# New order, engine and buffer tables for a hand-scheduled attention and SoLU kernel

## The chip, the cores and the metric

The kernel runs on one core of one Trainium2 chip. The metric is the time of one execution on the device in microseconds (us); the median of several runs counts. The engines are TensorE (PE, matmul; PEld is its weight load), VectorE (DVE), ScalarE (ACT), GpSimd (POOL) and SyncE (SP, which issues most of the transfers).

## What is computed

Attention with batch 4, 8 heads, 768 positions and head size 64, in which each position sees its last 96 positions and the first 8 ones, with a bias by distance and head; and then on its 3072 rows of 512 a feed-forward layer of width 1024 with a SoLU and a normalization. Cut to what matters:

```python
scores = q @ k.T / sqrt(64) - slope[head] * distance      # per batch and head
scores = where(local or first 8, scores, -1e9)
x = softmax(scores) @ v                                   # -> [3072, 512], all heads side by side
h = x @ w_in                                              # [3072, 1024]
solu = h * softmax(h)
ln = (solu - mean(solu)) / sqrt(var(solu) + 1e-6) * g_ln
out = ln @ w_out                                          # [3072, 512], float32
```

## The kernel before

The program is cut into 714 steps. Python code creates them with their dependencies (`Plan.step`), each with the engine or the engines that may do it. Four tables near the top of the file then decide: `ORDER` is the order in which all steps are written out, so each engine gets its own steps in that order and works through them in order; `SLOTS` gives each step the buffers that it takes; `ENGS` picks the engine of a step that has a choice; and `WARM` puts matmuls on constant data (L1292, tile busy) in front of some PE steps, where `20:2:13` means thirteen ahead of entry 20 of the order, into bank 2. `Plan.order` applies the tables. Waits follow from the dependencies and from who has the buffer.

For each of the 4 batches:

- q and k of a head pair are loaded (L523, tile x), cast to float16 (tile x again; L275 on ACT, L277 on DVE, L279 on POOL), transposed on PE (L785) and copied to kT and qT. For the last batch a transposing transfer does this (L530).
- A *scores* step makes the products of one head pair and half of the positions (L941), with the bias added by a matmul for batch 0 (L927). ACT takes the exponential (L949, tile eb). For batches 1 to 3 the bias is a factor instead, multiplied in by DVE or POOL (L959). The factor (tile fb) is made once by eight exponentials (L322) from distances and slopes (sf, L317).
- gscores and gexp do the first 8 positions (L998, L1013). *sums* adds up the weights (L1027), ACT takes the logarithm (L1044), DVE splits it (L1051), *spread* spreads it over the partitions (L1073), and ACT takes the reciprocal by an exponential (L1085, tile rr). av1 and av2 multiply by v (L1121), with a small copy (tick, L1129) between them, and DVE multiplies by rr to give xT (L1141).

For each of the 24 tiles of 128 rows: the first product gemm1 (L1174, 16 matmuls with their loads), the exponential ef (L1180, ACT), uu = ef * h (L1183, DVE), its squares (sq; L1190 on ACT or L1194 on DVE), a transpose of uu (L1209 on PE with a copy to tile late, or a transposing transfer, L1199), the second product gemm2 (L1266), the scaled output osb (L1276 on ACT, L1279 on DVE) and its store (L1283).

The weights: w_in is loaded in four pieces (L658, tile late) and cast in eight (w_in_sb). w_out is loaded in four pieces (L668), each of its eight blocks is scaled by g (gw; L681 on ACT, L683 on POOL, L687 on DVE), a product with a constant gives the mean over the rows (L694), and DVE subtracts it (L698, "centred"). The first gemm2 needs all eight centred blocks.

PE's results lie in eight banks of one tile, acc. A step takes one bank ("one") or a pair of banks ("big"), and gives it back when another engine has read it: a scores step's pair after ACT's exponential, a gemm1's pair only after ACT's exponential and DVE's uu, a gemm2's bank after the scaled output. In the code, for gemm1:

```python
g1 = step("PE", 1728, tt, xt_st[t] + w_in_st, None, take=("big", "ef"), mode="f", ...)
u = step("DVE", 1140, tt + 3000, [ex], None, take="uu", free=[g1], lat=113, name="u")
```

Of the kernel before, what the change touches and what calls it, by code (L numbers as in the profile page):

```python
# [30 lines left out]
FACT = {1, 2, 3}  # L31
SPLIT = False
ORDER = """
# [29 lines left out]
"""  # L63
SLOTS = """
# [10 lines left out]
"""  # L75
ENGS = """
# [5 lines left out]
"""  # L82
WARM = """
20:2:13 32:2:5 45:2:2 54:2:1 82:0:3 100:0:1 110:6:1 139:5:1 171:4:2
"""


# [1243 lines left out]
```

## Time and profile before

| what | before |
|---|---|
| median of 3 runs | 159.84 us (159.53 to 160.11) |
| the profiled execution's own time | 158.12 us |
| its span | 156.5 us, 4929 instructions |
| busy: PE, DVE, ACT, POOL | 144.1, 119.9, 123.8, 51.9 us |
| transfers | 35.83 MB, mean 229 GB/s |
| granted clock of TensorE | 1.00 over the span |

The profile is of one execution; its span leaves out what lies around the program. A busy time of PE includes the modelled ends of matmuls that overlap. "Idle before" names what ended the wait.

### The profile page before, as it was taken

To read this page: it belongs to the slowest core of one execution; us is meant where nothing else is said; L and a number is where in the kernel's file an instruction comes from. 1 tells how busy PE (TensorE), PEld (TensorE's weight loads), DVE (VectorE), ACT (ScalarE), POOL (GpSimd) and SP (SyncE) were. 2 spreads that over 40 slices of the span, in tenths; PEclk is the share of its full clock that TensorE was granted. 3 is DMA by queue.
4 is the path that set the end of the run, shared out by engine and by line. 5 is a ranking of instruction groups with operands and counts; after the bars stand their busy time and mean duration, and the time that the engine had idled before them with its cause. 6 is when DMAs were issued, how large, how long until landed. Compare 5 with 4: busy or idle time off the path is not lost.

```text
span 156.5 us, 4929 instructions
## 1 busy us (share of the span) xinstructions
PE 144.1 (92%) x1974; PEld 76.3 (49%) x1974; DVE 119.9 (77%) x249; ACT 123.8 (79%) x214; POOL 51.9 (33%) x120
## 2 busy tenths in 40 slices
PE   6998986997898999999998999999989799999991
PEld 2455553456454546556544456454444454445460
DVE  6966553799879998889999997499777462788840
ACT  3389986999996999758996998989999546589712
POOL 7705714189438521734960000448301000000000
PEclk9999999999999999999999999999999999999999
DMA  4997899999969999999999899999999983054684
GB/s 157 335 351 178 288 311 397 366 272 329 266 161 264 213 202 294 204 275 201 219 239 176 182 237 216 164 263 135 215 225 290 211 316 133 4 113 89 188 315 168
DMA packets 74317, 35.83 MB, mean 229 GB/s; under 512 B 63344, under 2 KB 69816, under 8 KB 74296
## 3 DMA queue, kind: packets, MB, share of 16 engines
q1 hardware_dynamic: 73576, 34.36, 92.8%
q10 hardware_dynamic: 720, 1.18, 2.0%
q8 instruction: 15, 0.25, 0.6%
q14 instruction: 6, 0.05, 0.1%
HBM read 23.15 MB, written 6.29 MB: 188 GB/s over the span
## 4 chain that ended last, share of the span: by engine, by line
PE 34%; DMA 21%; DVE 16%; SPq 13%; ACT 7%; issue 4%; POOL 3%; DVEq 0%; ACTq 0%; POOLq 0%
PE acc L1266 11%; PE acc L1174 10%; SPq L537 5%; DVE uu L1183 5%; DMA x<-in_k_dram 4%; DVE eb L959 4%; DMA x<-in_q_dram 4%; DMA kT<-x 4%; DMA vgn<-vgn 4%; PE acc L1121 4%; DMA out_dram<-w_out 3%; DVE sqv L1194 3%; SPq L523 3%; SPq L1199 3%; PE acc L785 2%
## 5 line engine op out<-in xcount | busy, mean ns | idle before, releaser
L1174 PE MATMUL acc<-w_in_sb,xT 128*128 128x512 f16 x192 | 44.0, 380 | 1.3 <-POOL w_in_sb L279 1.3
L1266 PE MATMUL acc<-gw_out_sb,late 128*128 128x512 f16 (+1 forms) x200 | 44.7, 371 | 0.0
L1183 DVE SCALAR_TENSOR_TENSOR uu<-ef,acc 128x1024 f16<-128x1024 f16 x24 | 29.1, 1216 | 6.3 <-ACT ef L1180 4.5
L949 ACT ACTIVATE eb<-acc 128x960 f16<-128x960 f32 (+1 forms) x32 | 29.3, 944 | 1.3 <-PE acc L941 1.1
L1180 ACT ACTIVATE ef<-acc 128x1024 f16<-128x1024 f32 x24 | 24.6, 1025 | 6.9 <-PE acc L1174 6.1
L1174 PEld LDWEIGHTS <-xT 128*128 128x128 f16 x192 | 17.8, 98 | 21.5 <-DVE g L625 1.2
L1266 PEld LDWEIGHTS <-late 128*128 128x128 f16 x200 | 18.4, 98 | 20.1 <-issue 0.6
L279 POOL CAST x<-x 128x768 f16<-128x768 f32 x19 | 17.0, 898 | 30.0 <-DMA qT<-x 17.0
L1141 DVE TENSOR_TENSOR xT<-acc,rr 128x768 f16<-128x768 f32 x16 | 15.1, 954 | 5.9 <-ACT rr L1085 4.5
L1276 ACT ACTIVATE w_out<-acc,rstd 128x512 f32<-128x512 f32 (+1 forms) x19 | 12.7, 678 | 7.5 <-PE acc L1266 4.3
L1190 ACT ACTIVATE sqa<-uu 128x1024 f16<-128x1024 f16 x14 | 14.8, 1058 | 1.8 <-DVE uu L1183 1.7
L959 DVE TENSOR_TENSOR eb<-eb,fb 128x960 f16<-128x960 f16 (+1 forms) x21 | 14.8, 735 | 0.0
L1085 ACT ACTIVATE rr<-acc 128x768 f32<-128x768 f32 x16 | 12.2, 805 | 2.9 <-PE acc L1073 2.8
L785 PE MATMUL acc<-ident,x 128*128 128x128 f16 x144 | 11.3, 220 | 2.1 <-POOL x L279 1.1
L1194 DVE SCALAR_TENSOR_TENSOR sqv<-uu 128x1024 f16<-128x1024 f16 x10 | 12.6, 1265 | 0.1
L1121 PE MATMUL acc<-eb,v 64*64 64x160 f16 (+2 forms) x448 | 12.5, 217 | 0.0
L1292 PE MATMUL acc<-busy 128*128 128x512 f16 x29 | 10.3, 485 | 1.5 <-DVE busy L598 1.5
L785 PEld LDWEIGHTS <-x 128*128 128x128 f16 x144 | 8.6, 98 | 5.6 <-POOL x L279 1.5
L1121 PEld LDWEIGHTS <-v 64*64 64x64 f16 x448 | 10.2, 107 | 2.2 <-issue 1.7
L941 PE MATMUL acc<-qT,kT 64*64 64x160 f16 (+2 forms) x384 | 10.8, 227 | 0.3 <-ACT qT L275 0.3
L279 POOL CAST v<-v 128x704 f16<-128x704 f32 (+3 forms) x13 | 6.9, 555 | 11.9 <-DMA v<-in_v_dram 11.9
L1121 PE MATMUL acc<-eg,vgz 64*64 64x192 f16 x128 | 9.2, 257 | 0.0
(113 smaller groups left out, 189.1 us busy)
## 6 DMA issues: line engine op xcount, KB each, us to landing
x<-in_k_dram SPq DMA_DIRECT2D x16, 384.0 KB, 5.8
x<-in_q_dram SPq DMA_DIRECT2D x16, 384.0 KB, 4.8
out_dram<-w_out SPq DMA_DIRECT2D x19, 256.0 KB, 2.9
v<-in_v_dram SPq DMA_DIRECT2D x12, 192.0 KB, 5.3
late<-in_moe_w_in_dram SPq DMA_DIRECT2D x4, 512.0 KB, 4.5
w_out<-in_moe_w_out_dram SPq DMA_DIRECT2D x4, 512.0 KB
v<-in_v_dram SPq DMA_DIRECT2D x12, 160.0 KB, 3.4
v<-in_v_dram SPq DMA_DIRECT2D x12, 96.0 KB, 6.9
```

What stands on the lines that cost most here:

```text
L279: nc.gpsimd.tensor_copy(out=out, in_=in_)
L785: nc.tensor.transpose(out=pt[:, ts(j, P)], in_=a[:, j], identity=ident)
L949: ex["fn"] = (lambda ex=ex, qk=qk, gw=gw: nc.scalar.activation(out=eb[at(qk, "eb")][:, :, 0:gw], in_=big(qk)[:, :, 0:gw], func=AF.Exp, sca ...
L959: eng.tensor_tensor(out=e, in0=e, in1=fb[:, p, :, 0:gw], op=ALU.mult)
L1121: nc.tensor.matmul(out=o_[:, gl : gl + m], lhsT=lhsT, rhs=rhs, start=(ph == 0 and (d, h) not in done), stop=(ph == 1 and last[d, h] == n), ...
L1141: nc.vector.tensor_tensor(out=xT[at(xt_own[b], "xT")][:, p : p + 2, q0:q1], in0=big(av)[:, :, 0:w], in1=rr[at(re, "rr")][:, :, 0:w], op=AL ...
L1174: nc.tensor.matmul(out=ph()[:, ts(fh, 512)], lhsT=xT[at(xt_own[b], "xT")][:, j, ts(t % NA, P)], rhs=w_in_sb[:, j, ts(fh, 512)], start=(j = ...
L1180: ex["fn"] = lambda g1=g1, t=t, ph=ph: nc.scalar.activation(out=ef[at(g1, "ef")], in_=ph(), func=AF.Exp, accum_out=s0[:, t : t + 1])
L1183: u["fn"] = lambda u=u, g1=g1, t=t, ph=ph: nc.vector.scalar_tensor_tensor(out=uu[at(u, "uu")], in0=ef[at(g1, "ef")], scalar=USC, in1=ph(), ...
L1190: nc.scalar.activation(out=sqs_["ACT"], in_=uu[at(u, "uu")], func=AF.Square, accum_out=s2[:, t : t + 1])
L1194: nc.vector.scalar_tensor_tensor(out=sqs_["DVE"], in0=uu[at(u, "uu")], scalar=1.0, in1=uu[at(u, "uu")], op0=ALU.mult, op1=ALU.mult, accum_ ...
L1266: nc.tensor.matmul(out=one(g2)[:, 0:wd], lhsT=uT[at(el_o, "uT")][:, c, :], rhs=gw_out_sb[:, c, sl_], start=(c == 0), stop=(c == NFC - 1))
```

## The change

In a few words: all orders, engines and buffers searched anew with a model in which TensorE's instruction fetches queue behind transfers. In the file only the four tables differ; the steps, their dependencies, the number of buffers, and what is computed stay as they are. The tables' rows tell a reader little; one or two lines of each:

```diff
 ORDER = """
-12 3 14 4 79 0 81 8 86 11 126 13 5 24 66 1 73 53 110 7 82 20 88 18 15 60 16 112 36 92 17 83 89 68 90
...
+3 14 13 4 15 12 60 2 0 53 99 92 86 17 62 115 66 16 18 1 24 23 101 63 8 102 19 110 126 73 55 5 94 56
...
 SLOTS = """
-0 0 0 2 3 2 4 0 1 5 1 3 4 0 0 2 2 5 0 0 0 1 2 1 2 0 1 2 5 0 6 0 2 2 7 2 10 0 0 1 4 6 0 3 3 0 1 1 1 1
...
+0 1 2 3 4 0 0 0 5 1 1 2 3 1 0 2 5 1 3 4 0 3 0 2 1 0 1 3 2 1 2 3 0 7 0 0 3 3 1 1 1 2 2 6 2 2 1 0 1 3
...
 ENGS = """
-0 0 0 1 0 2 1 2 1 1 0 2 1 1 1 1 0 1 0 0 1 0 1 1 2 1 0 2 2 2 1 1 2 2 0 0 1 1 0 1 0 2 0 0 0 1 0 1 0 1
...
+0 0 0 0 1 2 1 0 0 0 0 0 1 1 0 0 0 1 0 1 0 2 1 0 0 0 1 2 2 2 2 2 1 1 1 1 1 1 1 0 0 2 0 0 2 1 0 1 0 1
...
 WARM = """
-20:2:13 32:2:5 45:2:2 54:2:1 82:0:3 100:0:1 110:6:1 139:5:1 171:4:2
+23:6:13 25:6:6 34:6:2 46:7:4 47:0:1 57:7:1 66:7:2 73:4:1 110:6:4 116:4:2
 """
```

What the engine table does, by kind of step (ACT / DVE / POOL):

| step | before | change |
|---|---|---|
| cast of k and q (x) | 5 / 8 / 19 | 5 / 4 / 23 |
| copy to kT and qT | 15 / 9 / - | 11 / 13 / - |
| cast of v | 2 / 10 / 12 | 3 / 10 / 11 |
| cast of w_in | 3 / 1 / 4 | 1 / 2 / 5 |
| scaling of w_out (gw) | 3 / 3 / 2 | 1 / 7 / 0 |
| factor (L959) | - / 21 / 3 | - / 18 / 6 |
| squares | 14 / 10 / - | 17 / 7 / - |
| copy of a turned uu | 1 / 6 / - | 2 / 5 / - |
| scaled output | 19 / 6 / - | 15 / 10 / - |

Of POOL's factors one was in batch 1 and two in batch 3; now three are in batch 1, one in batch 2 and two in batch 3. WARM holds 29 matmuls before, two of them behind the first gemm1, and 36 now, all ahead of it.

What the order and buffer tables do to some PE steps of batches 1 to 3 (by step number; "held by" is who had the banks last, and what frees them; the count is of PE steps from the holder to the step):

| PE step | before: held by, freed by | change: held by, freed by |
|---|---|---|
| scores 357 | gemm1 774, uu (6) | scores 345, exponential (4) |
| scores 513 | gemm1 857, uu (3) | scores 501, exponential (3) |
| scores 672 | gemm1 954, uu (6) | scores 666, exponential (4) |
| sums 697 | gemm2 922, output on ACT (4) | gemm2 922, output on DVE (8) |
| scores 348 | scores 357, exponential (3) | gemm1 774, uu (5) |
| scores 498 | gemm1 823, uu (11) | gemm1 830, uu (6) |
| scores 510 | two turned q, copies (4) | gemm1 857, uu (7) |

Three places in the order, as the built programs have it.

SP, the first loads. Before, from the seventh x load to the last w_out load (x are pieces of q and k, v and vt of v, vgn the first 8 rows, late w_in):

```order
L523 DMA x_0_101<-in_k_dram 128x2x384
L523 DMA x_2_103<-in_q_dram 128x2x384
L537 DMA v_1_112<-in_v_dram 128x3x64
L545 DMA vt_89<-in_v_dram 64x4x64 x2
L537 DMA v_2_113<-in_v_dram 128x3x64
L537 DMA v_0_111<-in_v_dram 128x3x64
L537 DMA v_1_112<-in_v_dram 128x3x64
L537 DMA v_0_111<-in_v_dram 128x3x64
L537 DMA v_2_113<-in_v_dram 128x3x64
L552 DMA vgn<-in_v_dram 64x1x64
L658 DMA late<-in_moe_w_in_dram 128x1024 x4
L668 DMA w_out_71<-in_moe_w_out_dram 128x2x512 x4
```

In the change, from the first w_in load on (the eighth x load stands four rows ahead of this piece):

```order
L658 DMA late<-in_moe_w_in_dram 128x1024 x2
L545 DMA vt_89<-in_v_dram 64x4x64
L552 DMA vgn<-in_v_dram 64x1x64
L537 DMA v_2_113<-in_v_dram 128x3x64
L552 DMA vgn<-in_v_dram 64x1x64
L658 DMA late<-in_moe_w_in_dram 128x1024
L537 DMA v_0_111<-in_v_dram 128x3x64
L537 DMA v_2_113<-in_v_dram 128x3x64
L537 DMA v_0_111<-in_v_dram 128x3x64
L658 DMA late<-in_moe_w_in_dram 128x1024
L537 DMA v_1_112<-in_v_dram 128x3x64
L668 DMA w_out_71<-in_moe_w_out_dram 128x2x512
```

Three of the four w_in loads moved ahead of v pieces. Behind this piece a v piece, a w_out load, a k load of the next batch and the last two w_out loads follow; before, no other load stood between the last w_in and the last w_out.

ACT, its first rows. Before:

```order
L596 ACT_TABLE_LOAD
L275 CAST x_0_107<-x_0_101 128x768
L275 COPY kT_116<-acc 128x768
L275 CAST x_0_107<-x_1_102 128x768
L275 COPY qT_123<-acc 128x768
L275 COPY kT_117<-acc 128x768
L949 ACTIVATE eb_132<-acc 128x960
```

In the change:

```order
L596 ACT_TABLE_LOAD
L275 CAST x_0_107<-x_0_101 128x768
L322 ACTIVATE fb<-dm,sf 128x160 x8
L275 COPY kT_116<-acc 128x768
L275 COPY qT_121<-acc 128x768
L949 ACTIVATE eb_130<-acc 128x2x448
```

The factor's eight exponentials (L322), which stood behind the first three ef of batch 0, are now the second work of ACT.

DVE, from the second xT of batch 0 to the last centred block. Before:

```order
L1141 TENSOR_TENSOR xT_99<-acc,rr_147 128x2x384
L625 COPY g_73<-acc 128x8
L687 TENSOR_SCALAR gw_out_sb<-w_out_71,g_73 128x512 x3
L1183 SCALAR_TENSOR_TENSOR uu_151,s_93<-ef_148,acc 128x1024
L1183 SCALAR_TENSOR_TENSOR uu_152,s_93<-ef_149,acc 128x1024
L277 COPY late<-acc 128x1024 x2
L1183 SCALAR_TENSOR_TENSOR uu_153,s_93<-ef_150,acc 128x1024
L698 SCALAR_TENSOR_TENSOR gw_out_sb<-w_out_71,g_73,acc 128x512 x6
```

In the change:

```order
L1141 TENSOR_TENSOR xT_99<-acc,rr_147 128x2x384
L277 COPY fb<-fb 128x8x320
L687 TENSOR_SCALAR gw_out_sb<-w_out_71,g_73 128x512 x4
L1183 SCALAR_TENSOR_TENSOR uu_152,s_93<-ef_150,acc 128x1024
L687 TENSOR_SCALAR gw_out_sb<-w_out_71,g_73 128x512 x3
L1183 SCALAR_TENSOR_TENSOR uu_151,s_93<-ef_149,acc 128x1024
L1183 SCALAR_TENSOR_TENSOR uu_154,s_93<-ef_148,acc 128x1024
L698 SCALAR_TENSOR_TENSOR gw_out_sb<-w_out_71,g_73,acc 128x512 x2
L277 COPY late<-acc 128x1024
L698 SCALAR_TENSOR_TENSOR gw_out_sb<-w_out_71,g_73,acc 128x512 x3
```

Seven scalings of w_out stand on DVE where three stood, two uu now stand behind the last of them, and one copy of a turned uu instead of two stands among the centred blocks.

## Rows read from the trace of the kernel before

**Rows 1.** The page's first part: busy time, share of the span, instructions.
```profile
PE 144.1 (92%) x1974; PEld 76.3 (49%) x1974; DVE 119.9 (77%) x249; ACT 123.8 (79%) x214; POOL 51.9 (33%) x120
```

**Rows 2.** Table by stage: length; busy PE, PEld, DVE, ACT, POOL; clock; DMA share; GB/s.
```profile
0.00:25.40 25.40, 21.09 (x351) 11.60 (x352) 17.08 (x55) 18.08 (x25) 13.04 (x68) 1.00 0.87 279
25.40:40.40 15.00, 13.85 (x195) 8.21 (x195) 11.89 (x22) 14.40 (x29) 7.64 (x13) 1.00 1.05 336
40.40:60.00 19.60, 18.14 (x219) 9.12 (x216) 18.14 (x29) 17.69 (x31) 10.10 (x13) 1.00 1.03 221
60.00:80.00 20.00, 20.00 (x338) 11.80 (x335) 17.97 (x33) 16.39 (x27) 11.68 (x16) 1.00 1.15 236
80.00:130.80 50.80, 48.64 (x745) 24.29 (x742) 39.80 (x82) 42.35 (x76) 9.48 (x11) 1.00 1.11 221
```

**Rows 3.** Timeline of PE: start, length, instruction, count, idle before and what ended it.
```profile
25.36 5.34 PE L1174 MATMUL acc<-w_in_sb,xT 128*128 128x512 f16 x24 [1.26 <-POOL w_in_sb L279]
...
32.66 1.89 PE L694 MATMUL acc<-gw_out_sb,onesm 128*128 128x512 f16 x8
...
40.37 1.89 PE L1266 MATMUL acc<-gw_out_sb,late 128*128 128x512 f16 x8
...
43.16 0.84 PE L785 MATMUL acc<-ident,x 128*128 128x128 f16 x12 [0.57 <-POOL x L279]
...
50.66 0.22 PE L927 MATMUL acc<-bw,identb 64*64 64x64 f16 x2 [0.50 <-DVE uu L1183]
...
56.19 0.62 PE L1209 MATMUL acc<-ident,uu 128*128 128x128 f16 x8 [0.39 <-DVE uu L1183]
...
83.00 0.22 PE L927 MATMUL acc<-bw,identb 64*64 64x64 f16 x2 [0.59 <-DVE uu L1183]
...
115.56 0.22 PE L927 MATMUL acc<-bw,identb 64*64 64x64 f16 x2 [0.71 <-DVE uu L1183]
...
123.90 0.63 PE L1027 MATMUL acc<-eb,onesd 128*32 128x384 f16 x24 [0.86 <-ACT w_out L1276]
...
144.31 8.82 PE L1266 MATMUL acc<-gw_out_sb,late 128*128 128x512 f16 x48
```

**Rows 4.** The page's third part: the queue of PE's instructions; packets, MB, share.
```profile
q8 instruction: 15, 0.25, 0.6%
```

**Rows 5.** Timelines of POOL and ACT, where they wait for the weights' loads.
```profile
22.87 2.44 POOL L279 CAST w_in_sb<-late 128x512 f16<-128x512 f32 x4 [3.66 <-DMA late<-in_moe_w_in_dram]
30.57 2.04 POOL L683 TENSOR_TENSOR gw_out_sb<-w_out,g 128x512 f16<-128x512 f32 x2 [5.26 <-DMA w_out<-in_moe_w_out_dram]
...
24.67 0.62 ACT L275 CAST w_in_sb<-late 128x512 f16<-128x512 f32 x1 [0.73 <-DMA late<-in_moe_w_in_dram]
```

**Rows 6.** Timeline of ACT: its first copy, two scalings of w_out, the factor.
```profile
7.37 0.80 ACT L275 COPY kT<-acc 128x768 f16<-128x768 f16 x1 [2.55 <-PE acc L785]
...
25.97 1.33 ACT L681 ACTIVATE gw_out_sb<-w_out,g 128x512 f16<-128x512 f32 x2 [0.69 <-DMA w_out<-in_moe_w_out_dram]
...
32.64 2.66 ACT L322 ACTIVATE fb<-dm,sf 128x160 f16<-128x160 f32 x8
```

**Rows 7.** Timeline of DVE, 27 to 40 us.
```profile
27.22 0.49 DVE L687 TENSOR_SCALAR gw_out_sb<-w_out,g 128x512 f16<-128x512 f32 x1 [2.24 <-DMA w_out<-in_moe_w_out_dram]
...
29.62 1.22 DVE L1183 SCALAR_TENSOR_TENSOR uu<-ef,acc 128x1024 f16<-128x1024 f16 x1
...
31.90 1.49 DVE L277 COPY late<-acc 128x1024 f16<-128x1024 f16 x2
...
34.59 4.04 DVE L698 SCALAR_TENSOR_TENSOR gw_out_sb<-w_out,g,acc 128x512 f16<-128x512 f32 x6
...
39.34 0.74 DVE L698 SCALAR_TENSOR_TENSOR gw_out_sb<-w_out,g,acc 128x512 f16<-128x512 f32 x1
```

**Rows 8.** Line L959 (the factor): duration ns min/median/max, first and last start.
```profile
L959 DVE TENSOR_TENSOR eb<-eb,fb x21: 612/650/1987, 47.5 to 121.7; 128x960 f16<-128x960 f16 x11, 128x896 f16<-128x896 f16 x10
L959 POOL TENSOR_TENSOR eb<-eb,fb x3: 1875/2002/2273, 47.0 to 108.9; 128x896 f16<-128x896 f16 x2, 128x960 f16<-128x960 f16 x1
```

82 rows, old and new, of tables (ENGS, ORDER, SLOTS) are left out of this document.

## Prediction

> **What bounds the kernel now.** I read the totals first, then the table by stage, then TensorE's own rows with what ended each of its idle times, and last the rows of the engines that those waits name.
>
> TensorE (PE) is busy for 144.1 us of the span of 156.5 [rows 1]. By stage it is the bound in the middle: 20.00 of 20.00 us from 60 to 80 us, 48.64 of 50.80 from 80 to 130.8 [rows 2]. The end cannot move by itself: the last group of products starts at 144.31 us and runs through without a wait [rows 3], and the tail of the change holds the same products and transposes. So the kernel gains what PE no longer waits, and loses what it waits anew. Ahead of 25.4 us PE's 21.09 busy us [rows 2] hold the warm-up products, so its share says little there; the first product on the tokens starts at 25.36 us, after a wait of 1.26 us for the last cast piece of the first weight [rows 3]. From 25.4 to 40.4 ScalarE (ACT) has 14.40 of 15.00 us busy and VectorE (DVE) 11.89; from 40.4 to 60 DVE has 18.14 of 19.60 [rows 2].
>
> Behind the start-up, PE has five waits [rows 3]: 0.50, 0.59 and 0.71 us before a scores step (L927) for a uu of DVE, 0.39 us before a transpose (L1209) for its own uu, and 0.86 us before sums (L1027) for a scaled output of ACT. They add up to 3.05 us.
>
> **Part 1: the fetches.** The words of the change speak of PE's instruction fetches. The trace shows 15 packets of them, 0.25 MB [rows 4], and each idle row of PE that I found ends with a semaphore of ACT, DVE or POOL (GpSimd) [rows 3]. No idle time is left for a fetch to have caused, so both bounds of this term are 0. The Trainium skill, page "Runtime: NRT & Kernel Launch", section "Instruction fetch mechanics", says that an engine's sequencer fetches the next 16 KiB block over a queue of its own while the current one runs, so that the fetch is mostly hidden. By that rule the term is 0 as well, against the ground that the change gives for itself; how long a fetch stood in its queue no row shows.
>
> **Part 2: up to the first product (25.36 us).** SP issues the loads in another order, but ahead of the last w_in load stand the same pieces: eight x loads, eight v pieces, two vt, two vgn, three w_in. So it has the same bytes before it and lands at about 24.6 us again, where ACT's last cast had waited 0.73 us for it [rows 5]. It can land earlier: from 0 to 25.4 us the transfers ran at 279 GB/s, from 25.4 to 40.4 at 336 [rows 2], and three of the four w_in loads are now queued earlier, so the queue runs dry less. Half of that difference over the 15 us from 10 to 25 is (336 - 279) / 279 / 2 x 15 = 1.5 us, which I take as the most. Behind the landing POOL now casts three halves in a row (2.44/4 = 0.61 us each [rows 5], 1.8 us), where two engines shared them. The first product then starts between 24.6 + 1.8 = 26.4 and 24.9 us; I take 25.8, later by 0.4.
>
> The eight exponentials that build the factor (L322, 2.66 us) move from 32.64 us, in ACT's fullest stretch, to the second place on ACT, where it had been idle for 2.55 us ahead of 7.37 [rows 6]. Their input sf moves up on POOL with them. That idle time is the cover; without it ACT's first copy of kT, and all behind it, comes up to 2.66 us later, which would also show at the first product.
>
> **Part 3: from there to 44 us.** The mean of the second weight (L694) started at 32.66 us [rows 3]. It waited for POOL, which scaled two pieces in 2.04 us from 30.57 on, when their load had landed [rows 5]. Now DVE scales seven of the eight pieces, ACT one and POOL none; of the last load one is DVE's (0.49 us [rows 7]) and one ACT's (1.33/2 = 0.7 us [rows 6]), side by side. In the queue a k load of 384 KB and two v pieces (160 KB) now come ahead of the last w_out load: 0.54 MB, 1.6 us at 336 GB/s, against the up to 1.5 us of part 2. I take the same 30.57. The mean then starts at 30.6 + 0.7 + 0.2 = 31.5 us, 1.2 earlier. The three products ahead of it take 5.3 us [rows 3], from 25.8 to 31.1, and do not hold it.
>
> DVE is next: the first second product (L1266, 40.37 us [rows 3]) needs all eight centred pieces (L698). After its last scaled piece, at 31.1 us, DVE has two uu (1.2 each), eight centred pieces (4.04/6 = 0.67 each) and one copy of a turned tile (1.49/2 = 0.7) [rows 7]: 2.4 + 5.4 + 0.7 = 8.5, so 39.6 us, where the last centred piece ended at 39.34 + 0.74 = 40.1 [rows 7]. That is 0.5. Six instead of five transposed x tiles now stand ahead of that product, so the wait of 0.57 us for POOL at 43.16 us [rows 3] loses its place. Together 1.1 to 1.2 us; I take 1.2. ACT does not bound this stretch any more: it loses the 2.66 us and two scalings (1.4), and takes over one tile copy and two x casts. If the w_out load lands 1.6 us later, DVE ends at 41.2 and the part costs 0.5 us; if it lands 1.5 us earlier, the part gains 2.2.
>
> **Part 4: the rest.** The table of banks in the section on the change shows what four of the five later waits hung on. Three scores steps took banks that a first product had held, so they stood behind ACT's exponential and DVE's uu; now each takes banks that only the exponential of an earlier scores step frees. The sums step took the bank of a second product four PE steps before; now it is eight. So 0.50 + 0.59 + 0.71 + 0.86 = 2.66 us [rows 3] lose their cause. What is late next: other steps now stand behind a uu, as the same table shows for scores steps 348, 498 and 510; 348 most, with the least PE work between. I put three new waits at the mean of the five, 3.05/5 = 0.61: 1.8 us. Net -0.8; the bounds are -2.7 (no new wait) and +2.0 (the slower rival).
>
> The seven more warm-up products (36 for 29) stand ahead of the first product, where PE waits for others, and cost 0; if that cover were gone, each is a product of 512 columns, 5.34/24 = 0.22 us [rows 3], 1.6 us in all. The squares, outputs and casts that change engines count where an engine bounds; PE bounds after 60 us, so I cost them at 0 there. If ACT or DVE fell behind, they would show as new waits, which part 4 holds.
>
> **Sum.** -1.2 (part 3, which swallows the +0.4 of part 2) and -0.8 (part 4): -2.0 on a span of 156.5, so 154.5 us, and 156.1 for the profiled execution, whose own time is 158.12. The median of the three runs is 159.84, 1.72 above it; there the forecast is **157.8 us**. About 0.3% (0.5 us) is what a measurement can tell from no change.
>
> **Rivals.**
> - *More is gained.* No new wait takes the place of the four (-2.7) and the w_out load lands early (-1.8): -4.5, 155.3 us. For it speaks that the four waits have lost their cause; against it, that three steps now stand behind a uu. Chance 0.18.
> - *Nothing is gained.* The w_out load lands 1.6 us later (+0.5) and new waits leave -0.5 of part 4: 159.8 us. This is also the case in which the change does only what its words say, where the trace shows nothing to gain. Chance 0.14.
> - *Slower: POOL's factors.* POOL multiplies six score tiles by the factor instead of three. One takes POOL 1.88 to 2.27 us; DVE's take 0.65 as a median and 1.99 at the longest [rows 8], so the two engines stretch each other. It decides from 40.4 to 60 us, where DVE is nearly full [rows 2] and POOL has three factors for one. If two of DVE's multiplies there are stretched by 1.99 - 0.65 = 1.34 us, 2.7 us of DVE come late, each uu behind them holds its banks longer, and PE has five more waits of 0.6 us (2.9) on top of the three: part 4 is -2.7 + 1.8 + 2.9 = +2.0. Part 3 keeps half, -0.6: +1.4, 161.2 us. Two stretched multiplies are the point; with one the forecast holds. Chance 0.22. The Trainium skill, page "SBUF — State Buffer", section "Who interferes with whom", says that a DVE instruction with two SBUF inputs contends with a GpSimd instruction that reads SBUF, and that one of the two is blocked in full. The 1.99 us agrees with that; by this rule each pair that meets is such a case.
>
> **How the numbers follow.** The forecast (156.8 to 159.3) has the remaining 0.46. Faster by over 0.3% is 0.46 + 0.18 = 0.64, within 0.3% 0.14, slower 0.22. The range goes from 155.8, half way into the larger gain, to 160.9, most of the way into the slower case.
>
> **What would show it.** Right: L694 starts near 31.5 us and the first L1266 near 39.8; the three scores waits for uu and that of L1027 are gone from their steps; the last group of products starts near 142.3. Part 3 is wrong if the scaling on DVE shows a longer wait for w_out; part 4, if PE's waits for uu sum to over 3 us again. The slower rival shows as DVE rows of L959 near 2 us between 40 and 60 us with PE idle behind them. Part 1 is wrong if idle time went that no engine had ended.

## The result: 1.3% slower, and the profile after

| what | before | after |
|---|---|---|
| median, 20 executions each, same chip | 159.22 us | 160.14 us |
| ratio after / before | | 1.0128 [1.0085, 1.0170] |
| the profiled execution's own time, span | 158.12, 156.5 us | 159.42, 157.4 us |

The ratio is taken over the undisturbed executions of each kernel alone (the profiles of e4, e5, e10 and e12 are of disturbed ones, so single waits are read in them, not their spans). It is 1.28% of 159 us, 2.0 us slower; the medians of all 20 lie only 0.9 us apart, so the sign is firmer than the size. The forecast was 2.0 us faster; the measured interval (1.4 to 2.7 us slower) holds the 1.4 us of the slower rival, though not for that rival's reason.

The page's busy times and the queue of instructions after the change, for [rows 1, 4]:

```profile
PE 145.7 (93%) x1981; PEld 78.2 (50%) x1981; DVE 122.9 (78%) x248; ACT 121.0 (77%) x210; POOL 59.0 (37%) x125
...
q8 instruction: 15, 0.25, 0.6%
```

The table by stage after, for [rows 2] (same columns), and one stretch of its own:

```profile
0.00:25.40 25.40, 21.69 (x339) 12.14 (x340) 14.45 (x50) 16.96 (x28) 15.51 (x71) 1.00 0.94 278
25.40:40.40 15.00, 13.23 (x140) 7.36 (x140) 12.61 (x24) 12.23 (x21) 5.90 (x12) 0.89 1.02 334
80.00:130.80 50.80, 48.95 (x702) 24.13 (x703) 42.98 (x81) 42.83 (x77) 13.57 (x13) 1.00 1.17 215
...
27.95:31.37 3.42, 3.42 (x9) 1.22 (x8) 1.87 (x5) 1.33 (x3) 0.00 (x0) 0.50 1.09 370
```

PE's timeline after, for [rows 3]:

```profile
25.77 0.26 PE L1121 MATMUL acc<-eb,v 64*64 64x160 f16 x2 [0.57 <-DVE tick L1129]
27.55 7.03 PE L1174 MATMUL acc<-w_in_sb,xT 128*128 128x512 f16 x24 [0.82 <-DVE xT L1141]
34.75 1.89 PE L694 MATMUL acc<-gw_out_sb,onesm 128*128 128x512 f16 x8
43.25 1.89 PE L1266 MATMUL acc<-gw_out_sb,late 128*128 128x512 f16 x8
45.94 0.39 PE L1174 MATMUL acc<-w_in_sb,xT 128*128 128x512 f16 x1
...
56.19 0.57 PE L1027 MATMUL acc<-eb,onesd 128*32 128x384 f16 x16 [0.68 <-DVE uu L1183]
87.48 1.89 PE L1266 MATMUL acc<-gw_out_sb,late 128*128 128x512 f16 x8 [0.82 <-DVE uu L1183]
110.97 1.89 PE L1174 MATMUL acc<-w_in_sb,xT 128*128 128x512 f16 x8 [1.03 <-DVE uu L1183]
```

The two inputs of the first product. DVE before, and then DVE and POOL of the change:

```profile
23.95 0.96 DVE L1141 TENSOR_TENSOR xT<-acc,rr 128x768 f16<-128x768 f32 x1 [0.23 <-ACT w_in_sb L275]
```

```profile
25.23 0.42 DVE L277 CAST w_in_sb<-late 128x512 f16<-128x512 f32 x1
25.68 1.82 DVE L1141 TENSOR_TENSOR xT<-acc,rr 128x768 f16<-128x768 f32 x2
...
25.40 1.83 POOL L279 CAST w_in_sb<-late 128x512 f16<-128x512 f32 x3 [3.76 <-DMA late<-in_moe_w_in_dram]
```

Three things stand in these rows. The first product comes 2.2 us later, and what ended its wait is xT, the end of the first attention group on DVE, no longer a cast of w_in. Both inputs are late, though: xT ended at 24.91 us before and at 27.50 now, the casts of w_in at 25.31 [rows 5] and at 27.24. Its three tiles take 7.03 in place of 5.34 us: the clock stood at 0.50, the 1.2 GHz level, from 27.95 to 31.37 us, behind small products and two idle times of PE. And the mean follows the products at once, where it had waited for w_out.

ACT's timeline shows where the attention group lost its time:

```profile
5.94 2.66 ACT L322 ACTIVATE fb<-dm,sf 128x160 f16<-128x160 f32 x8 [1.20 <-POOL sf L317]
9.75 0.80 ACT L275 COPY kT<-acc 128x768 f16<-128x768 f16 x1 [1.16 <-PE acc L785]
...
12.46 2.65 ACT L949 ACTIVATE eb<-acc 128x896 f16<-128x896 f32 x3 [1.20 <-PE acc L941]
16.48 0.80 ACT L275 COPY kT<-acc 128x768 f16<-128x768 f16 x1 [1.37 <-PE acc L785]
```

ACT's first copy starts at 9.75 us, where before it was 7.37 [rows 6], and ACT waits three times for PE. PE works in order: the tile of k that the copy at 9.75 us takes was cast by 7.02 us, but transposed only from about 9.2 us on, behind warm-up products and the transpose of a piece that landed later; before 16.48 us the transpose of the last x piece stood ahead of scores whose inputs were there.

For one comparison through all runs I cut each profile at the start of the fourth first product (45.94 us after, 43.84 before, as this row of before shows): the **head** is what lies ahead, the **rest** is the span less that start, 112.7 us before and 111.5 after.

```profile
43.84 1.89 PE L1174 MATMUL acc<-w_in_sb,xT 128*128 128x512 f16 x8
```

### The profile page after: what moved, and what is told of

It reads as the page before. It is cut to its first block, busy times and chain, and to the rows that moved or that the text cites. A ratio compares the mean times of both kernels' runs of the same rounds, so it can differ in the third digit from the quotient of the medians.

```text
span 157.4 us, 4948 instructions
## 1 busy us (share of the span) xinstructions
PE 145.7 (93%) x1981; PEld 78.2 (50%) x1981; DVE 122.9 (78%) x248; ACT 121.0 (77%) x210; POOL 59.0 (37%) x125
## 4 chain that ended last, share of the span: by engine, by line
PE 60%; DVE 16%; issue 7%; ACT 6%; DMA 4%; SPq 3%; POOL 1%; DVEq 0%; ACTq 0%; POOLq 0%
PE acc L1266 24%; PE acc L1174 18%; PE acc L1121 7%; DVE uu L1183 5%; DMA x<-in_q_dram 4%; DVE sqv L1194 4%; PE acc L785 3%; ACT eb L949 3%; DVE eb L959 2%; PE acc L1027 2%; SPq L523 2%; PE acc L941 2%; PE acc L1073 1%; DVE qT L277 1%; POOL x L279 1%
## 5 line engine op out<-in xcount | busy, mean ns | idle before, releaser
L1174 PE MATMUL acc<-w_in_sb,xT 128*128 128x512 f16 x192 | 45.6, 390 | 1.9 <-DVE uu L1183 1.0
L1266 PE MATMUL acc<-gw_out_sb,late 128*128 128x512 f16 (+1 forms) x200 | 44.7, 371 | 0.8 <-DVE uu L1183 0.8
L1180 ACT ACTIVATE ef<-acc 128x1024 f16<-128x1024 f32 x24 | 24.6, 1024 | 13.6 <-PE acc L1174 13.5
L279 POOL CAST x<-x 128x768 f16<-128x768 f32 x23 | 20.3, 889 | 38.3 <-DMA kT<-x 12.7
L949 ACT ACTIVATE eb<-acc 128x896 f16<-128x896 f32 (+1 forms) x32 | 28.9, 948 | 1.8 <-PE acc L941 1.8
L1266 PEld LDWEIGHTS <-late 128*128 128x128 f16 x200 | 18.5, 98 | 20.8 <-issue 1.8
L1190 ACT ACTIVATE sqa<-uu 128x1024 f16<-128x1024 f16 x17 | 18.0, 1056 | 0.1
L959 POOL TENSOR_TENSOR eb<-eb,fb 128x896 f16<-128x896 f16 (+1 forms) x6 | 13.0, 2179 | 6.0 <-ACT eb L949 4.8
L959 DVE TENSOR_TENSOR eb<-eb,fb 128x960 f16<-128x960 f16 (+1 forms) x18 | 14.0, 796 | 0.0
L1276 ACT ACTIVATE w_out<-acc,rstd 128x512 f32<-128x512 f32 (+1 forms) x15 | 10.0, 672 | 5.1 <-PE acc L1266 4.9
L1292 PE MATMUL acc<-busy 128*128 128x512 f16 x36 | 12.2, 471 | 1.5 <-DVE busy L598 1.5
L1121 PE MATMUL acc<-eb,v 64*64 64x160 f16 (+3 forms) x448 | 12.1, 217 | 0.6 <-DVE tick L1129 0.6
L1194 DVE SCALAR_TENSOR_TENSOR sqv<-uu 128x1024 f16<-128x1024 f16 x7 | 11.8, 1693 | 0.1
```

The costliest lines, as they stand in the source:

```text
L279: nc.gpsimd.tensor_copy(out=out, in_=in_)
L949: ex["fn"] = (lambda ex=ex, qk=qk, gw=gw: nc.scalar.activation(out=eb[at(qk, "eb")][:, :, 0:gw], in_=big(qk)[:, :, 0:gw], func=AF.Exp, sca ...
L959: eng.tensor_tensor(out=e, in0=e, in1=fb[:, p, :, 0:gw], op=ALU.mult)
L1121: nc.tensor.matmul(out=o_[:, gl : gl + m], lhsT=lhsT, rhs=rhs, start=(ph == 0 and (d, h) not in done), stop=(ph == 1 and last[d, h] == n), ...
L1174: nc.tensor.matmul(out=ph()[:, ts(fh, 512)], lhsT=xT[at(xt_own[b], "xT")][:, j, ts(t % NA, P)], rhs=w_in_sb[:, j, ts(fh, 512)], start=(j = ...
L1180: ex["fn"] = lambda g1=g1, t=t, ph=ph: nc.scalar.activation(out=ef[at(g1, "ef")], in_=ph(), func=AF.Exp, accum_out=s0[:, t : t + 1])
```

## The experiments

All ratios are against the kernel before, run beside on the same chip.

### The halves exchanged (e1, e2)

Each edit joins the tables of the two kernels at one place in the order:

```diff
 e1  ORDER, ENGS, SLOTS, WARM up to scores step 354:  before;  from there: the change
 e2  ORDER, ENGS, SLOTS, WARM up to gemm1 step 781:   the change;  from there: before
```

> Order, engines and banks are those of the kernel before up to the scores step 354 (246 of 714 steps), and those of the change for the rest; 7 bank numbers and a few places at the seam differ. Theory A (the change loses at its head, up to the first product, and gains in the rest): the product gemm1:774 starts near 43.8 us as before, the rest keeps the 1.5 us that the two traces show between it and the last gemm1, so 0.8 to 1.5 us faster than the kernel before (ratio 0.990 to 0.995). Theory C (POOL's factors and the loaded port cost the time, in the rest): as slow as the change or between the two, 0 to 2 us slower than before.

> The other half: order, engines and banks of the change up to gemm1:781 (261 steps), those of the kernel before for the rest (4 bank numbers differ). Theory A: the first product starts near 27.5 us, the late head is not given back, 2.0 to 3.5 us slower than before (ratio 1.013 to 1.022), so slower than the change itself or equal to it. Theory C: at most 1 us slower than before.

Measured: e1 1.0033 [0.9976, 1.0090], e2 1.0182 [1.0113, 1.0251]. PE's timelines at the first product and at the cut, e1 and then e2:

```profile
24.86 5.34 PE L1174 MATMUL acc<-w_in_sb,xT 128*128 128x512 f16 x24 [1.53 <-POOL w_in_sb L279]
...
42.80 1.89 PE L1174 MATMUL acc<-w_in_sb,xT 128*128 128x512 f16 x8
```

```profile
28.32 5.34 PE L1174 MATMUL acc<-w_in_sb,xT 128*128 128x512 f16 x24 [0.98 <-DVE xT L1141]
...
45.02 1.90 PE L1174 MATMUL acc<-w_in_sb,xT 128*128 128x512 f16 x8
```

The loss goes with the head: with the head of before, the change is not told apart from before (at most 0.9% slower), and with its own head it is slower, the two intervals apart. The gain for the rest that one pair of traces showed did not come, though: theory A had given e1 0.8 to 1.5 us. By the profiles, the rest of the change took 111.3 to 113.0 us (after, e1, e3, e6, e7, e8, e11; mean 112.2), the rest of before 112.7 and 112.7 (before, e2) and 113.4 (e9): a gain of some 0.7 us inside a spread of 1.7. The cut came at 45.0 to 46.0 us with the unmended head of the change (after, e2, e3, e6) and at 42.8 to 43.8 with that of before (before, e1, e9): 2.5 us later by the means.

### The clock (e3)

```diff
-... 110:6:4 116:4:2
+... 110:6:4 116:4:2 148:4:4
```

> The change with four warm-up products of 512 columns more, right ahead of the first product, in the 1.2 us in which TensorE waits there. Theory B (the lower clock level from 27.95 to 31.37 us comes from TensorE's idle times and small products ahead of it, and costs 1.28 us by itself): the granted clock stays at 1.0 through the first product, which takes 1.73 us in place of 3.01, and the run is 0.8 to 1.3 us faster than the change. Rival: the level falls whatever stands right there, because the thin stretch from 20 us on has already decided it, or the time is given back to a later wait: within 0.4 us of the change.

Measured: 1.0164 [1.0108, 1.0219], no faster than the change, although the clock over the span stayed above 0.995 in five of its six executions. In its profile the clock stays at full level and the three tiles take 5.34 us, but the first product starts at 28.73 us, so the mean came at 34.25, only 0.5 us ahead of the change's profile:

```profile
27.01 0.26 PE L1121 MATMUL acc<-eb,v 64*64 64x160 f16 x2 [1.63 <-DVE tick L1129]
28.73 5.34 PE L1174 MATMUL acc<-w_in_sb,xT 128*128 128x512 f16 x24
34.25 1.89 PE L694 MATMUL acc<-gw_out_sb,onesm 128*128 128x512 f16 x8
```

Three profiles whose heads differ by the four warm-up products alone (after, e2, e3) start the first product at 27.55, 28.32 and 28.73 us: single profiles differ by over 1 us there, and xT ended just ahead of it in each (27.50, 28.27, 28.69), so the warm-up products did not hold it. The last section has a part of the reason. The lower level is not the change's alone either: over the whole span the clock was below 0.995 in 14 of 20 executions of the change and in 29 of 51 of the kernel before (and in all 17 of e4, e8 and e12, so a part of what these three lose is the clock's). Theory B falls as the cause of the slowdown; the 1.7 us that the level cost in that one profile is real.

### POOL's factors (e4)

The factor steps go back to the engines of before, by `ENGS` alone: 344, 353, 356, 497 and 653 to DVE, 341 and 668 to POOL.

> The change with the factor multiplies on the engines of the kernel before (three on POOL in place of six; the order is the change's). Theory C: VectorE is no longer stretched (the factor's longest below 1.3 us, the sum of squares back to 1.27 us), 1 to 2 us faster than the change. Theory A: within 0.5 us of the change, on either side, since the head is untouched.

Measured: 1.0288 [1.0237, 1.0340], the opposite of theory C, and more than theory A allowed. One place shows a wait that the change does not have, on DVE, POOL and PE:

```profile
119.70 3.46 DVE L959 TENSOR_TENSOR eb<-eb,fb 128x960 f16<-128x960 f16 x2
...
120.37 2.28 POOL L959 TENSOR_TENSOR eb<-eb,fb 128x896 f16<-128x896 f16 x1
...
123.22 0.50 PE L1027 MATMUL acc<-eb,onesd 128*32 128x384 f16 x10 [2.27 <-DVE eb L959]
```

Two multiplies on DVE take 3.46 us beside one on POOL, where two of them take 1.3 alone, and PE waits 2.27 us for them. So the mechanism of the slower rival exists, at about the price that it named (2.2 us for two multiplies, where it took 2.7). The wait costs again behind it: from 123.2 to 127.0 us the granted clock was 0.57. But the change had put this very step (668) on DVE, and of its six POOL factors none ends a wait of PE in the rows above. The Trainium skill, page "SBUF — State Buffer", section "Who interferes with whom", says that such a pair contends and that the contention is an exclusive lock. The trace agrees: 1.3 us of work and the 2.28 us of POOL come to 3.6, beside the 3.46 measured.

### The two limbs ahead of the first product (e5, e6, e7)

A limb is here a chain of work that ends at the first product: the attention group, which gives xT, or the weight w_in with its casts.

e5, pieces of `ORDER` (56 and 82 are transposes of k, 102 of q; 199 is a scores step, 200 its exponential):

```diff
-63 8 102 19 110 126 73 55 5 94 56 95
+63 8 19 55 56 102 110 126 73 5 94 95
...
-82 173
+199 82 173
...
-83 105
+200 83 105
```

e6 (139 is the last w_in load, 120 a v load, 134 and 142 casts of w_in); e7 is both:

```diff
-127 84 120
+127 139 84 120
...
-129 222 142
+129 222 134 142
```

> The change with two moves in its head. On TensorE the transpose turn_k:56 (its piece lands third from first) goes ahead of the six warm-up products and of turn_q:102; the scores step 199 and its exponential 200, whose inputs are there at 11.3 us, go ahead of turn_k:82 and its copy on ScalarE, which wait for the last load of x. Theory A1 (the first product is late by two limbs of one length: the attention that feeds xT:224, which ended at 27.50 us, and the weight w_in with three casts on POOL, which ended at 27.24): ScalarE's idle 1.37 us ahead of 16.48 shrinks below 0.5 and the last exponential ends 1.0 to 1.4 us earlier, but the first product comes only 0.2 to 0.4 us earlier, since the other limb holds it; within 0.5 us of the change. Rival A2 (only the attention limb counts): the first product and the run come 1.0 to 1.4 us earlier.

> The change with the other limb alone: SP issues the last w_in load ahead of the v load for whose buffer it waited 1.55 us (issue at about 16.2 in place of 19.2 us), and POOL casts the half that had landed long before ahead of the two of that load. Theory A1: the casts end at 24 to 25 us, the first product stays where xT:224 holds it, 0 to 0.3 us earlier; the run within 0.5 us of the change. Rival A3 (only the weight limb counts, as the prediction had it): the first product and the run come 1.0 us or more earlier.

> Both moves together. Theory A1: the first product starts 1.0 to 1.5 us earlier than in the change, and the run is 0.7 to 1.5 us faster than the change, which leaves it 0.5 to 1.3 us behind the kernel before. If neither limb sets the end (the time is decided behind the head): within 0.4 us of the change.

Measured: e5 1.0069 [1.0020, 1.0117], e6 1.0142 [1.0085, 1.0198], e7 1.0123 [1.0039, 1.0207]. ACT and PE of e5, then POOL and PE of e6:

```profile
8.51 0.78 ACT L275 COPY kT<-acc 128x768 f16<-128x768 f16 x1
12.19 3.61 ACT L949 ACTIVATE eb<-acc 128x896 f16<-128x896 f32 x4 [2.22 <-PE acc L941]
16.20 0.80 ACT L275 COPY kT<-acc 128x768 f16<-128x768 f16 x1 [0.40 <-PE acc L785]
...
27.04 5.34 PE L1174 MATMUL acc<-w_in_sb,xT 128*128 128x512 f16 x24 [0.82 <-DVE xT L1141]
37.06 0.51 PE L785 MATMUL acc<-ident,x 128*128 128x128 f16 x6 [1.81 <-POOL x L279]
46.26 1.90 PE L1174 MATMUL acc<-w_in_sb,xT 128*128 128x512 f16 x8
```

```profile
22.60 2.62 POOL L279 CAST w_in_sb<-late 128x512 f16<-128x512 f32 x4
...
29.26 5.34 PE L1174 MATMUL acc<-w_in_sb,xT 128*128 128x512 f16 x24 [0.82 <-DVE xT L1141]
```

In e6 the casts end at 25.2 us, 2 us earlier than in the change, and the first product gains nothing: A3, that the weights alone hold it, is out. It is no clean test of the weights, for the v load that went behind w_in came later too: DVE's cast of v starts at 24.38 us there, at 21.25 in the change, and the attention ends later with it. In e5 the last exponential ends 1.1 us earlier (21.38 for 22.46 us), but the first product starts at 27.04 us, 0.5 us ahead of the change's profile, with w_in's casts ending at 26.74. That is nearer to A1, two limbs of one length, than to A2. In e7 it starts at 27.44, no earlier than in e5; A1 had given the two moves 1.0 to 1.5 us. So the attention limb ends last in each of these profiles, with the weights 0.2 to 0.3 us ahead of it in the change and in e5, and no move tried here is shown to give the lateness back. The timed gain of e5 is some 0.6% with overlapping intervals, and e7 adds none. Behind the first product something else waited: in e5 PE idles 1.81 us at 37.06 for a cast of x, in e7 0.52 and 0.84 us:

```profile
27.44 5.34 PE L1174 MATMUL acc<-w_in_sb,xT 128*128 128x512 f16 x24 [0.82 <-DVE xT L1141]
35.36 0.51 PE L785 MATMUL acc<-ident,x 128*128 128x128 f16 x6 [0.52 <-POOL x L279]
42.35 0.51 PE L785 MATMUL acc<-ident,x 128*128 128x128 f16 x6 [0.84 <-POOL x L279]
45.38 1.90 PE L1174 MATMUL acc<-w_in_sb,xT 128*128 128x512 f16 x8
```

### The loads of x (e11)

On top of e7, in `ORDER` (266 and 273 load the first x tiles of the second batch; 146 is a w_out load):

```diff
-122 114 184 146
+122 114 266 273 184 146
```

> The change with both limbs mended (e7) and the first two x loads of the second sequence moved ahead of the four w_out loads on SP. In e7 the first product came 0.9 us earlier than in the runs with the same order without the moves, and it was lost again between the mean and the first L1266, where TensorE waited 0.52 and 0.84 us for POOL casts of x loads that had just landed. Theory A4 (those loads are the next limit behind the first product): both waits go, the product gemm1:774 starts 0.8 to 1.3 us earlier than in e7 (45.4 us), the run is 0.5 to 1.2 us faster than e7. Rival (VectorE's centred blocks, which ended at 41.6 us in e7, or the w_out loads that now land later hold it): gemm1:774 within 0.4 us of e7.

Measured: 1.0106 [1.0028, 1.0184], as e7. PE's timeline:

```profile
25.00 0.39 PE L1121 MATMUL acc<-eb,v 64*64 64x160 f16 x12 [0.70 <-DVE v L277]
29.04 5.34 PE L1174 MATMUL acc<-w_in_sb,xT 128*128 128x512 f16 x24 [0.82 <-DVE xT L1141]
45.74 1.90 PE L1174 MATMUL acc<-w_in_sb,xT 128*128 128x512 f16 x8
```

Both waits for x are gone, as A4 said, and the cut did not move (45.74 for 45.38): now PE waits for a v piece and the first product is 1.6 us later. That fits a load queue that is full: the transfers' share is 0.94 up to 25.4 us and 1.02 behind it. What goes ahead in the queue is paid for by what stands behind. It is one profile, and a part of the 1.6 us can be its scatter. The run shows no gain, where A4 had 0.5 to 1.2 us.

### Parts of the change alone (e8, e9, e12, e10)

e8, from the change, and e9, from the kernel before (21 is the factor's exponentials, 22 the copy that repeats them, 19 their input, 8 the constants of the sums):

```diff
 e8
-95 103 21 9 ... 189 224 22 156 ... 276 748 270
+95 103 9 ... 189 224 156 ... 276 748 21 22 270
 e9
-81 8 86 ... 92 17 83 ... 52 2 28 ... 131 19 139 ... 738 21 152
+81 19 86 ... 92 17 21 83 ... 52 2 8 28 ... 131 139 ... 738 152
```

e12, from the kernel before: the entries of `ENGS` for the eight scalings of w_out (0 ACT, 1 DVE, 2 POOL). e10 is e1 with the edit of e9.

```diff
-2 2 0 0 1 1 0 1
+1 1 1 1 1 1 1 0
```

> One part of the change undone: the eight exponentials that build the factor go back to ScalarE's stretch at 32 us, behind the third first exponential, and the copy that repeats them behind them on VectorE. The prediction's price (their new place lies in idle time and costs 0, the old one bound ScalarE): the first product stays within 0.2 us, the run is 0 to 1 us slower than the change. Rival: their new place delays ScalarE's first copies (the first copy of kT started 1.16 us after they ended, so there is slack): then the first product comes up to 1 us earlier and the run is faster than the change.

> One part of the change done alone in the kernel before: the eight exponentials of the factor go into ScalarE's idle time ahead of its first copy of kT, with their input ahead of the sums' constants on POOL; nothing else moves. In the change, putting them back cost 3 us (e8). Theory S (they bound ScalarE at 32 us in either order): the copies, exponentials and PE's waits behind 34.7 us come 1 to 2.6 us earlier, the run is 0.5 to 2 us faster than before. Theory V (in the order of before VectorE, full from 28.8 to 40.1 us with scalings, uu, copies and centred blocks, sets the first L1266 at 40.4 us, and ScalarE's gain waits for it): the first L1266 moves by less than 0.5 us and the run is within 0.5 us of before.

> Another part of the change alone in the kernel before: the eight scalings of w_out on the engines of the change (seven on VectorE, one on ScalarE, none on POOL), in the order of before. The prediction's part 3: the mean starts near 31.5 to 31.9 us in place of 32.66 and the first L1266 near 39.6 to 39.9, the run is 0.5 to 1 us faster than before. Theory V: VectorE, which has no idle time from 28.8 to 40.1 us, takes four more scalings of 0.49 us, the uu behind them come later, the mean starts no earlier than 32.2 and the first L1266 0 to 1 us later; the run is 0 to 1 us slower.

> The first hybrid (head of before, rest of the change) with the factor's exponentials early as in e9: the version in which every part that has shown a gain stands. Theory S: 0.5 to 2 us faster than the kernel before. Theory V: within 0.6 us of the kernel before, as e1 was.

Measured: e8 1.0321 [1.0241, 1.0400], e9 0.9965 [0.9909, 1.0022], e12 1.0264 [1.0181, 1.0348]; e10 gave no ratio (six executions from 157.56 to 162.31 us) and stays open. ACT and PE of e8; ACT and PE of e9; DVE and PE of e12:

```profile
34.71 2.65 ACT L322 ACTIVATE fb<-dm,sf 128x160 f16<-128x160 f32 x8
...
28.32 5.34 PE L1174 MATMUL acc<-w_in_sb,xT 128*128 128x512 f16 x24 [0.98 <-DVE xT L1141]
38.09 0.61 PE L1209 MATMUL acc<-ident,uu 128*128 128x128 f16 x8 [2.03 <-ACT kT L275]
```

```profile
4.99 2.66 ACT L322 ACTIVATE fb<-dm,sf 128x160 f16<-128x160 f32 x8
34.46 0.80 ACT L275 COPY kT<-acc 128x768 f16<-128x768 f16 x1 [1.98 <-PE acc L785]
...
39.92 1.89 PE L1266 MATMUL acc<-gw_out_sb,late 128*128 128x512 f16 x8
```

```profile
30.72 3.03 DVE L687 TENSOR_SCALAR gw_out_sb<-w_out,g 128x512 f16<-128x512 f32 x6 [5.52 <-DMA w_out<-in_moe_w_out_dram]
...
34.94 1.04 PE L1209 MATMUL acc<-ident,uu 128*128 128x128 f16 x8 [3.62 <-DVE uu L1183]
37.48 3.54 PE L694 MATMUL acc<-gw_out_sb,onesm 128*128 128x512 f16 x8
```

In the order of the change the early factor is worth about 3 us (1.0321 less 1.0128, 1.9%, the clock's part in it), at no cost to the first product: e8's starts at 28.32 us too. In the order of before it is worth at most 0.9%: ACT gets its 2.66 us back and waits 1.98 of them for PE, and the first L1266 moves by 0.45 us, as theory V said. e9 has the lowest ratio of all versions and clearly beats the change, but it is not told apart from the kernel before. In e12 the six scalings stand on DVE ahead of every uu and wait 5.52 us for w_out; PE gets its uu 3.62 us late, and in the table by stage the clock is 0.79 from 25.4 to 40.4 us. That is worse than theory V had it: I had counted the scalings' 0.49 us each, and not their wait.

## Why the prediction was wrong, step by step

- **Part 1, fetches: right.** 15 packets again, and no idle time that a fetch would explain.
- **Part 2, the first product: wrong, and this decided the sign.** It took w_in's landing and three casts as what holds it, and came to 25.8 us, 26.4 at the latest. The three casts took 1.83 us, as forecast, but the landing was taken as unmoved (24.6 us) and came at 25.4: SP, after 1.55 us of waiting for a v buffer, issued the last w_in load only at 19.20 us. The casts so ended at 27.24, and this limb alone lies outside the forecast. The other limb, the attention group, was left out of the sum, and it ended later still: the prediction followed the factor's exponentials on ACT, but not PE's order of transposes and scores, nor ACT behind it. ACT's first copy was 2.4 us later, the group's last exponential ended at 22.46 us, and xT at 27.50. That the loss lies in the head is shown by e1 and e2; these two ends are read from the traces, and no run took the loss back by mending them. How it divides between the order of the loads and that of the engines stays open.
- **Part 2, the factor's exponentials in ACT's idle time: right.** e8 shows no cost at the head. The price of 0 for the warm-up products was not tested alone; six of them stood ahead of the transpose that e5 moved forward.
- **Part 3: right in what it removed, wrong in what it hung on.** In the change's profile w_out no longer holds the mean. But the mean is held by the products, which the prediction had let end at 31.1 us. At full clock the mean comes 5.5 us behind the first product (e2, e3), where before it was 7.3 [rows 3]: of the lateness, 1.8 us are given back here. From its last scaled piece to its last centred block DVE then took 8.6 us (34.37 to 42.99), where 8.5 were forecast: that sum was right, but it began at 34.4 in place of 31.1 us, since the last three scalings stood behind a uu of the late first product. e12 shows the assumption under it: a scaling on DVE is cheap only if its load has landed, or every uu waits with it.
- **Part 4: right in size in that profile, not firm.** The five waits of 3.05 us became three of 0.68, 0.82 and 1.03, 2.53 in all: three new waits as forecast, 0.84 each where 0.61 was taken, though not at the steps that it named. Timed, e1 shows no gain.
- **The slower rival: the sign, not the cause.** POOL's factors are in the change's favour (e4).

The sum by profiles: about +2.5 at the cut and -0.7 in the rest make +1.8, beside the timed +2.0 (0.9 by the medians).

## What to carry to other kernels

Before pricing a wait that ends at a join, write down every chain that ends there, with when each ends; a term for one chain is worth nothing while another ends 0.3 us ahead of it. In this start-up, whose transfers ran almost without a gap, moving a load forward only chose who waits (e6, e11). When work is moved to a faster engine, price the wait that it carries into that engine's queue, not its duration.

## What the runs showed that was not expected

- A second price of a wait: behind an idle time of PE the granted clock could fall to the 1.2 GHz level. In the change, 0.57 and 0.82 us idle and small products, and then three tiles in 7.03 us for 5.34; in e12, 3.62 us idle, and then the mean in 3.54 us for 1.89; in e4, 2.27 us idle, and then the clock at 0.57. In e2, with two idle times of 0.98 us at the same place, it stayed at 1.00, so these runs do not say when it falls.
- The two limbs meet on DVE, and this is a part of the scatter of the first product. In the change two casts of w_in stand in DVE's queue ahead of the last tick and xT. The second took 0.42 us in the change's profile, where it began ahead of POOL's casts of w_in (25.23 and 25.40 us, above), and 0.83 us in e2, e3 and e4, where it began behind their start; in e5, e6, e7 and e11, where it began ahead of them or behind their end, it took 0.41 or 0.42. So a pair of casts on the two engines stretches as well, not the factors alone. DVE and POOL of e2:

```profile
25.64 0.83 DVE L277 CAST w_in_sb<-late 128x512 f16<-128x512 f32 x1
...
25.43 2.07 POOL L279 CAST w_in_sb<-late 128x512 f16<-128x512 f32 x3 [3.25 <-DMA late<-in_moe_w_in_dram]
```

- The gain of the rest that the first pair of traces showed (1.2 us) lay inside the spread of 1.7 us between profiles.
